# Linear attention block: the last VectorE step of a Q unit's feature map, issued in front of or behind the division of the token tile that follows it

## The chip, the cores and the metric

The kernel runs on one core of one Trainium2 chip. The metric is the device time of one launch in microseconds (us), the span of the core and the launch's own overhead together; the profile shows the span alone, some 1.8 us less.

## The reference, cut to what matters

```python
def _A_ref(x, wqkv, wo):                 # 32 heads of 32, S = 2048, D = 1024
    q, k, v = ...                        # x @ wqkv, split into heads
    phi = lambda t: jnp.where(t > 0, t + 1, jnp.exp(t)) + 1e-6
    pq, pk = phi(q), phi(k)
    kv = jnp.einsum("bhsd,bhse->bhde", pk, v)
    z = jnp.einsum("bhsd->bhd", pk)
    num = jnp.einsum("bhqd,bhde->bhqe", pq, kv)
    den = jnp.einsum("bhqd,bhd->bhq", pq, z)[..., None] + 1e-6
    return (num / den) ... @ wo
xn = layernorm(x)
out = x + _A_ref(xn, ...) * silu(swiglu_ffn(xn, w_gate, w_up, w_down))
```

## The kernel before

The kernel goes through three stages: K, V and the sums kv and z (0 to about 128 us); Q, the numerators and denominators, and the product with wo (128 to 250 us); then the SwiGLU part (250 to 762 us), which begins with the gate and up weights. The change is in the second stage. Its Q units (128 columns of q for 512 tokens, eight matmuls into one PSUM bank `q_ps`) belong to one of four blocks of 512 tokens, and their result goes through the feature map `emit_phi`. With `act=True`, three ScalarE activations are followed by one VectorE addition:

```python
def emit_phi(work, t_ps, dst, W, in_place=False, act=False):
    e_t = work.tile([P, W], FP32, name="e_t", tag="e_t")          # two buffers
    if act:
        nc.scalar.activation(out=e_t[:], in_=t_ps, func=ACT.Relu, scale=-1.0)
        nc.scalar.activation(out=e_t[:], in_=e_t[:], func=ACT.Exp, scale=-1.0)
        nc.scalar.activation(out=t_ps, in_=t_ps, func=ACT.Relu)
        nc.vector.scalar_tensor_tensor(out=dst, in0=e_t[:], scalar=EPS, in1=t_ps,
                                       op0=ALU.add, op1=ALU.add)
        return
    ...

def emit_Q(b, g):
    ...                                                     # eight matmuls into q_ps
    emit_phi(phiw, q_ps[:], pqT[:, g, :], TB, in_place=True, act=b > 0)
```

A token tile (128 tokens) takes eight short matmuls into `nd`, which holds numerators and denominators, and a division on VectorE. `nd` has one buffer of three PSUM banks, so the next tile's matmuls wait until this division has read it:

```python
def emit_ND(b, t, nd):
    for g in range(G):
        nc.tensor.matmul(nd[:, j, gi, :], lhsT=pqT[:, g, ttok], rhs=KVZ[:, g, :], ...)
    ...                                                     # two tensor_scalar: rden = den + EPS
    nc.vector.reciprocal(out=rden[:, 0:G, :], in_=rden[:, 0:G, :])
    for j in range(NJ):                                     # three multiplies: o_sb = nd * rden
        nc.vector.tensor_tensor(...)
```

The loop over blocks puts tiles among the Q units of the next block and the products with wo (`s_ps`) of the block before. In block 0 there is a tile after every second Q unit. `nd_item` in blocks 1 to 3 also carries a step of the weight preparation (on VectorE: `w_sb` times a power of two).

```python
for b in range(NB):
    q = [q_item(b + 1, g) for g in range(G)] if b + 1 < NB else []
    sl = sh(b - 1, 0) + sh(b - 1, 1) if b > 0 else []
    body = q[:2] + mix(q[2:], sl)
    at = (1, 4, 7, 10) if len(body) > 12 else ((1, 3, 5, 7) if b == 0 else (0, 2, 4, 6))
    for k, f in enumerate(body):
        f()
        if k in at:
            nd_item(b, at.index(k))()
```

In the third stage raw up-weights are loaded by DMA while the stage runs. Each is first read by a ScalarE activation that sums its squares, in the same ScalarE stream that empties the PSUM banks of the running products:

```python
def emit_st0(key, t):
    ...
    nc.scalar.activation(out=junk, in_=raw_view(key, t), func=ACT.Square, accum_out=asum[:])
...
load_w_to(...)                                              # step i of the up-weight loop
pipe(i + 4)                                                 # simplified: emit_st0 of a weight four steps ahead
if first and i in range(6, 11):
    io_load(mb)                                             # x and s for the output stage, 128 KB each
```

Of the kernel before, what the change touches and what calls it, by code (L numbers as in the profile page):

```python
# [10 lines left out]
ALU = mybir.AluOpType  # L11
# [10 lines left out]
def kernel(  # L22
# [11 lines left out]
    nc = tc.nc  # L34
# [24 lines left out]
    EPS = 1e-6  # L59
# [72 lines left out]
    hsc = persist.tile([P, 3], FP32, name="hsc")  # L132
    chs, rch, hmx = hsc[:, 0:1], hsc[:, 1:2], hsc[:, 2:3]

    def emit_phi(work, t_ps, dst, W, in_place=False, act=False):
        e_t = work.tile([P, W], FP32, name="e_t", tag="e_t")
        if act:
            nc.scalar.activation(out=e_t[:], in_=t_ps, func=ACT.Relu, scale=-1.0)
            nc.scalar.activation(out=e_t[:], in_=e_t[:], func=ACT.Exp, scale=-1.0)
            nc.scalar.activation(out=t_ps, in_=t_ps, func=ACT.Relu)  # L140
            nc.vector.scalar_tensor_tensor(out=dst, in0=e_t[:], scalar=EPS, in1=t_ps,
                                           op0=ALU.add, op1=ALU.add)
            return
        nc.scalar.activation(out=e_t[:], in_=t_ps, func=ACT.Exp)
        if in_place:
            r = t_ps
            nc.vector.tensor_scalar(out=r, in0=t_ps, scalar1=0.0, scalar2=EPS, op0=ALU.max, op1=ALU.add)  # L147
        else:
            r_t = work.tile([P, W], FP32, name="r_t", tag="r_t")
            r = r_t[:]  # L150
            nc.scalar.activation(out=r, in_=t_ps, func=ACT.Relu)
            nc.vector.tensor_scalar(out=r, in0=r, scalar1=EPS, scalar2=None, op0=ALU.add)
        nc.vector.scalar_tensor_tensor(out=dst, in0=e_t[:], scalar=1.0, in1=r,  # L153
                                       op0=ALU.min, op1=ALU.add)
# [8 lines left out]
    def emit_Q(b, g):  # L163
        if b not in pqT_tiles:
            pqT_tiles[b] = blk12.tile([P, G, TB], BF16, name="pqT", tag="pqT")
        pqT = pqT_tiles[b]
        btok = slice(b * TB, (b + 1) * TB)
        q_ps = ps2.tile([P, TB], FP32, name="q_ps", tag="B2")
        for dc in range(DC):
            nc.tensor.matmul(q_ps[:], lhsT=wq_sb[:, dc, g * P:(g + 1) * P], rhs=xn_ap(dc, btok),  # L170
                             start=(dc == 0), stop=(dc == DC - 1))
        emit_phi(phiw, q_ps[:], pqT[:, g, :], TB, in_place=True, act=b > 0)
# [136 lines left out]
    def prep_step(between=None):  # L309
        key = prep_q.popleft() if prep_q else None  # L310
        t = None
        if key is not None:
            t = w_slot()
            load_gu(t, key[1], key[2])
        if prep_out:
            emit_store(*prep_out.popleft(), nc.sync)
        k3 = prep_st.popleft()
        if prep_st[1] is not None:
            emit_st0(*prep_st[1])
        if k3 is not None:  # L320
            emit_st1(k3[0], stat_ps[0]())
        if between is not None:
            between()
        if k3 is not None:
            emit_st2(*k3)
            emit_T(*k3, later=True)
            prep_out.append(k3)
            if k3[0] in gkeys[0:2]:
                w_tiles[k3[0]] = k3[1]
        prep_st.append((key, t) if key is not None else None)  # L330
# [12 lines left out]
    def psa_tile(name):  # L343
        t = psA.tile([P, NJ, 512], FP32, name=name, tag="A")
        return t, t[:, :, 0:GPT * NDW].rearrange("p j (g c) -> p j g c", c=NDW)

    kvz_ps = psa_tile("kvz")[1]
    with ExitStack() as p1:
# [164 lines left out]
        def emit_Bev(i, c):  # L513
            kv_ps = kv_banks.pop((i, c))
            if i not in pkv_tiles:
                pk_sb = work.tile([P, D], BF16, name="pk_sb", tag="pk_sb")
                pkv_tiles[i] = (pk_sb, v_bufs[i % 2])
            pk_sb, v_sb = pkv_tiles[i]
            if c < NCC:
                emit_phi(phiw, kv_ps[:], pk_sb[:, c * CW:(c + 1) * CW], CW, in_place=i >= 9)  # L520
            else:
                vc = c - NCC
                nc.scalar.copy(out=v_sb[:, vc * GPC:(vc + 1) * GPC, 0:P],
                               in_=kv_ps[:].rearrange("p (g c) -> p g c", c=P))
# [78 lines left out]
        for j in range(NJ):  # L603
# [3 lines left out]
                                    in1=mask[:, None, :].to_broadcast([P, ng, P]), op=ALU.mult)  # L607
            nc.vector.tensor_tensor(out=KVZ[:, g0:g0 + ng, P:P + HPG],
                                    in0=kvz_ps[:, j, 0:ng, P:P + 1].to_broadcast([P, ng, HPG]),
                                    in1=sel[:, None, :].to_broadcast([P, ng, HPG]), op=ALU.mult)  # L610
# [23 lines left out]
    with ExitStack() as p2:  # L634
# [9 lines left out]
        def emit_ND(b, t, nd):  # L644
            pqT = pqT_tiles[b]
            ttok = slice(t * P, (t + 1) * P)
            if b not in o_blks:
                o_blks[b] = blk.tile([P, TPB, D], BF16, name="o_blk", tag="o_blk")
            o_sb = o_blks[b][:, t, :]
            for g in range(G):  # L650
                j, gi = divmod(g, GPT)
                nc.tensor.matmul(nd[:, j, gi, :], lhsT=pqT[:, g, ttok], rhs=KVZ[:, g, :], start=True, stop=True,  # L652
                                 skip_group_check=True)
            rden = small.tile([P, NJ * GPT, HPG], FP32, name="rden", tag="rden")
            for j0, j1, ng in ((0, NJ - 1, GPT), (NJ - 1, NJ, G - (NJ - 1) * GPT)):
                nc.vector.tensor_scalar(
                    out=rden[:, j0 * GPT:(j1 - 1) * GPT + ng, :].rearrange("p (j g) h -> p j g h", j=j1 - j0),
                    in0=nd[:, j0:j1, 0:ng, P:P + HPG], scalar1=EPS, scalar2=None, op0=ALU.add)
            nc.vector.reciprocal(out=rden[:, 0:G, :], in_=rden[:, 0:G, :])
            for j in range(NJ):  # L660
                g0 = j * GPT
                ng = min(GPT, G - g0)
                nc.vector.tensor_tensor(
                    out=o_sb[:, g0 * P:(g0 + ng) * P].rearrange("p (g h e) -> p g h e", g=ng, h=HPG),
                    in0=nd[:, j, 0:ng, 0:P].rearrange("p g (h e) -> p g h e", h=HPG),
                    in1=rden[:, g0:g0 + ng, :, None].to_broadcast([P, ng, HPG, DH]),
                    op=ALU.mult)

        def emit_OT(b, t):
            if t == 0:  # L670
                oT_tiles[b] = otp.tile([P, G, TB], BF16, name="oT", tag="oT")
            nc.sync.dma_start_transpose(out=oT_tiles[b][:, :, t * P:(t + 1) * P], in_=o_blks[b][:, t, :])
# [17 lines left out]
        def q_item(b, g):  # L690
            return lambda: emit_Q(b, g)
# [4 lines left out]
        def nd_item(b, t):  # L696
            def f():
                raw, nd = psa_tile("nd")

                def nd_ot():  # L700
                    emit_ND(b, t, nd)
                    emit_OT(b, t)
                if b > 0 and (b < NB - 1 or t % 2 == 0):
                    stat_ps[0] = lambda: raw[:, 0, 511:512]
                    prep_step(nd_ot)
                else:
                    nd_ot()
            return f

        def mix(a, b_):  # L710
            r = []
            for k in range(max(len(a), len(b_))):
                r += a[k:k + 1] + b_[k:k + 1]
            return r

        def sh(b, hf):
            return [s_item(b, t, cc) for t in (2 * hf, 2 * hf + 1) for cc in range(NCC)]
# [7 lines that stand above are left out]
                f()  # L725
                if k in at:
                    nd_item(b, at.index(k))()
        b = NB - 1
        blk_es.close()
        blk12_es.close()  # L730
# [519 lines left out]
```

## Time and profile before

Median 764.8 us of three runs (764.25 to 765.98); the profiled execution has a span of 762.1 us. Two lines of the page of the kernel before, its busy times by engine and the engines' shares of the chain that ended last:

```profile
...
PE 752.7 (99%) x3731; PEld 350.4 (46%) x3731; DVE 543.6 (71%) x1026; ACT 348.3 (46%) x479; POOL 269.1 (35%) x382
...
PE 94%; DVE 2%; DMA 1%; ACT 1%; issue 1%; SPq 0%; ACTq 0%; DVEq 0%
...
```

TensorE (PE) is busy practically always, and the chain is almost all PE. PE's busy time is no proof that it works at its peak; here what counts is that hardly any gap is left. The table of windows of the kernel before (each row: window, its length, busy time of PE, PEld, VectorE = DVE, ScalarE = ACT and GpSimd = POOL, granted clock, DMA share, GB/s):

```profile
...
core 0: us, PE busy (x) PEld busy (x) DVE busy (x) ACT busy (x) POOL busy (x), PEclk, DMA share, GB/s
145.00:166.00 21.00, 18.82 (x117) 9.30 (x115) 15.34 (x36) 16.57 (x30) 3.26 (x3) 1.00 0.40 82
166.00:240.00 74.00, 74.00 (x417) 36.41 (x416) 49.00 (x129) 54.06 (x86) 46.28 (x40) 1.00 0.93 262
...
```

From 166 to 240 us PE has no gap; between 145 and 166 us it lacks more than 2 us. The list of PE's waits of the kernel before (what waited, for what; total us, times, longest):

```profile
...
PE nd L652 <- DVE o_blk L663: 1.7, 2, 1.2
...
PE kv_ps L508 <- DMA wkv_sb<-in_A_wqkv_dram: 0.8, 1, 0.8
PE nd L652 <- DVE pqT L153: 0.4, 1, 0.4
...
```

The first line is the one that the change aims at. PE's own timeline of block 0 before (start, duration, line, operation, count; in brackets the idle time and what ended it). A row of 16 is two Q units, a row of 8 one tile:

```profile
...
147.01 3.62 PE L170 MATMUL q_ps<-xnT,wq_sb 128*128 128x512 bf16 x16
151.79 0.64 PE L652 MATMUL nd<-KVZ,pqT 128*128 128x132 bf16 x8 [1.17 <-DVE o_blk L663]
152.28 3.62 PE L170 MATMUL q_ps<-xnT,wq_sb 128*128 128x512 bf16 x16
...
156.20 3.62 PE L170 MATMUL q_ps<-xnT,wq_sb 128*128 128x512 bf16 x16
160.39 0.64 PE L652 MATMUL nd<-KVZ,pqT 128*128 128x132 bf16 x8 [0.58 <-DVE o_blk L663]
160.87 3.62 PE L170 MATMUL q_ps<-xnT,wq_sb 128*128 128x512 bf16 x16
...
```

Eight matmuls of a Q unit take 1.73 us and the eight of a tile 0.47, so the pairs could start 3.45 + 0.47 = 3.92 us apart. They start at 147.01, 152.28, 156.20, 160.87 and (not shown) 164.90. The first pair takes 5.27 us and so loses 1.35; its bracket shows only 1.17, because the row's end is modelled (3.62 us after its start), and the next matmul could have started after 3.45. VectorE's timeline over the first of these gaps (L141 is the addition, L656 to L663 the division):

```profile
...
147.45 0.69 DVE L141 SCALAR_TENSOR_TENSOR pqT<-e_t,q_ps 128x512 bf16<-128x512 f32 x1 [0.56 <-ACT q_ps L140]
149.11 0.69 DVE L141 SCALAR_TENSOR_TENSOR pqT<-e_t,q_ps 128x512 bf16<-128x512 f32 x1 [0.97 <-ACT q_ps L140]
149.71 0.25 DVE L656 TENSOR_SCALAR rden<-nd 128x24 f32<-128x24 f32 x2
...
150.38 1.35 DVE L663 TENSOR_TENSOR o_blk<-nd,rden 128x384 bf16<-128x384 f32 x3
151.65 0.68 DVE L141 SCALAR_TENSOR_TENSOR pqT<-e_t,q_ps 128x512 bf16<-128x512 f32 x1
```

The tile's matmuls had ended at 147.17 us (last one started 146.94, 0.23 us long), but its division starts at 149.71, right behind an addition for which VectorE had sat idle. The chain of waits in this stretch, followed back from PE, has the same story in order of time (start, duration, what):

```profile
...
147.35 0.59 ACT e_t L138
...
149.11 0.69 DVE pqT L141
149.80 0.17 DVE rden L656 x2
...
150.38 1.36 DVE o_blk L663 x3
...
151.79 0.64 PE nd L652 x8
...
```

| from the profile before | us |
|---|---|
| span | 762.1 |
| PE idle between 145 and 166 us | 2.18 |
| waits of nd on the division | 1.17 and 0.58 |
| one Q unit on ScalarE (three activations) | about 1.7 |
| the addition | 0.69 |
| the division, first start to the next instruction's start | 1.94 |

The Trainium skill, "Perfetto Trace Analysis", section "Optimization Strategy", says to look for the gaps of the engine in question and find the semaphore and the instruction that end them. That is what these views do; this trace bears it out, with the 1.17 us gap on the division leading to the addition's wait of 0.97 us for ScalarE.

### The profile page before, as it was taken

How to read it: one execution, taken by the hardware profiler on the slowest of the kernel's cores; microseconds unless marked ns; L12 is line 12 of the kernel's file. 1: busy time of each engine (PE TensorE's matmuls, PEld its weight loads, DVE VectorE, ACT ScalarE, POOL GpSimd, SP SyncE). 2: the span in 40 equal slices, each digit the busy share in tenths (PEclk: the TensorE clock that was granted, in tenths of full speed). 3: DMA queues.
4: the chain of work that ended last, by engine and by line, in shares of the span. 5: the costliest groups of instructions: out<-in, count | busy, mean ns of one | idle time of the engine just before them, and what ended most of it. 6: DMA issues, size and time to landing. Idle time of an engine off the chain costs nothing.

```text
span 762.1 us, 10455 instructions
## 1 busy us (share of the span) xinstructions
PE 752.7 (99%) x3731; PEld 350.4 (46%) x3731; DVE 543.6 (71%) x1026; ACT 348.3 (46%) x479; POOL 269.1 (35%) x382
## 2 busy tenths in 40 slices
PE   8999999999999999999999999999999999999997
PEld 3444444444444444444444444444444444444444
DVE  7788676876656588888889885358676767787335
ACT  4545777688853566666448411132323222211022
POOL 0577699708563255868655000110000000200000
PEclk9999999999999999999999999999999999999999
DMA  9986799669889769897887237398654445530824
GB/s 315 302 151 125 204 298 319 248 139 286 238 263 263 250 231 308 290 359 289 314 310 281 86 86 260 116 355 329 228 190 177 166 165 170 170 144 15 281 81 136
DMA packets 105908, 170.29 MB, mean 223 GB/s; under 512 B 34688, under 2 KB 82176, under 8 KB 95232
## 3 DMA queue, kind: packets, MB, share of 16 engines
q1 hardware_dynamic: 99280, 143.81, 59.9%
q0 software_dynamic: 3984, 21.24, 7.0%
q10 hardware_dynamic: 2592, 4.59, 1.8%
q8 instruction: 29, 0.48, 0.3%
q14 instruction: 23, 0.19, 0.1%
HBM read 111.67 MB, written 50.59 MB: 213 GB/s over the span
## 4 chain that ended last, share of the span: by engine, by line
PE 94%; DVE 2%; DMA 1%; ACT 1%; issue 1%; SPq 0%; ACTq 0%; DVEq 0%
PE zw L754 25%; PE kv_ps L508 14%; PE xb L754 13%; PE dzw L939 12%; PE s_ps L682 7%; PE yb L754 6%; PE dx L939 6%; PE q_ps L170 4%; PE dy L939 3%; DMA wkv_sb<-in_A_wqkv_dram 1%; PE kvz L530 1%; PE nd L652 1%; PE df L939 1%; DVE pqT L153 1%; DVE q_ps L147 1%
## 5 line engine op out<-in xcount | busy, mean ns | idle before, releaser
L754 PEld LDWEIGHTS <-w_sb 128*128 128x128 f16 (+1 forms) x1568 | 152.2, 98 | 182.9 <-issue 0.2
L508 PE MATMUL kv_ps<-wkv_sb,xnT 128*128 128x512 bf16 x512 | 113.7, 379 | 1.5 <-DMA wkv_sb<-in_A_wqkv_dram 0.8
L754 PE MATMUL xb<-xnT,w_sb 128*128 128x512 bf16 x448 | 115.0, 379 | 0.0
L754 PE MATMUL zw<-xnT,w_sb 128*128 128x512 bf16 x448 | 105.8, 379 | 0.0
L754 PE MATMUL zw<-S,w_sb 128*128 128x512 f16 x448 | 105.8, 379 | 0.0
L280 POOL TENSOR_TENSOR w_sb<-w_sb 128x512 f16<-128x512 bf16 x42 | 49.2, 1172 | 118.5 <-ACT s_sb L685 31.4
L247 ACT ACTIVATE w_sb<-w_sb 128x2048 bf16<-128x2048 bf16 x42 | 79.9, 1902 | 8.4 <-DMA w_sb<-in_B_w_up_dram 5.6
L939 PE MATMUL dx<-w_sb,hT 128*128 128x512 bf16 x210 | 79.6, 379 | 0.0
L508 PEld LDWEIGHTS <-xnT 128*128 128x128 bf16 x512 | 48.5, 97 | 57.1 <-issue 1.5
L939 PEld LDWEIGHTS <-hT 128*128 128x128 bf16 (+1 forms) x462 | 45.2, 98 | 51.7
L170 PE MATMUL q_ps<-xnT,wq_sb 128*128 128x512 bf16 x256 | 58.5, 379 | 0.2 <-DVE pqT L153 0.2
L939 PE MATMUL dzw<-w_sb,hT 128*128 128x512 f16 x196 | 58.3, 379 | 0.0
L682 PE MATMUL s_ps<-wo_sb,oT 128*128 128x512 bf16 x256 | 57.8, 379 | 0.0
L754 PE MATMUL yb<-S,w_sb 128*128 128x512 f16 x224 | 57.4, 378 | 0.0
L782 DVE SCALAR_TENSOR_TENSOR s<-yb,rc_all,s 128x512 f32<-128x512 f32 x42 | 31.5, 749 | 35.1 <-ACT s L781 35.0
L830 ACT ACTIVATE sg<-cg 128x1024 bf16<-128x1024 f32 x28 | 29.6, 1057 | 57.4 <-DVE cg L823 57.4
L823 DVE SCALAR_TENSOR_TENSOR cg<-zw,rc_all,s 128x1024 f32<-128x1024 f32 x28 | 35.9, 1284 | 25.9 <-PE zw L754 14.0
L283 POOL TENSOR_TENSOR w_sb<-w_sb 128x512 f16<-128x512 bf16 x42 | 50.8, 1210 | 0.0
L281 POOL TENSOR_TENSOR w_sb<-w_sb 128x512 f16<-128x512 bf16 x42 | 49.5, 1178 | 3.3
L282 POOL TENSOR_TENSOR w_sb<-w_sb 128x512 f16<-128x512 bf16 x42 | 50.3, 1198 | 0.0
L879 POOL TENSOR_TENSOR hs<-hT 128x512 f16<-128x512 bf16 x2 | 2.5, 1254 | 132.6 <-ACT sg L830 132.6
L913 POOL DMA_DIRECT2D out_dram<-io x16 | 8.7, 542 | 101.9 <-DVE io L912 101.6
(152 smaller groups left out, 1082.0 us busy)
## 6 DMA issues: line engine op xcount, KB each, us to landing
w_sb<-pk_g SPq DMA_DIRECT2D x27, 1024.0 KB, 5.6
pk_g<-w_sb SPq DMA_DIRECT2D x14, 1024.0 KB, 5.2
w_sb<-wd SPq DMA_DIRECT2D x14, 1024.0 KB, 5.0
w_sb<-pk_u SPq DMA_DIRECT2D x14, 1024.0 KB, 4.9
pk_u<-w_sb POOLq DMA_DIRECT2D x13, 1024.0 KB, 6.1
w_sb<-wd SPq DMA_DIRECT2D x14, 768.0 KB, 5.9
w_sb<-in_B_w_gate_dram SPq DMA_DIRECT2D x14, 512.0 KB, 6.4
w_sb<-in_B_w_down_dram SPq DMA_DIRECT2D x28, 256.0 KB, 3.9
```

Of the source, the lines that this page charges most:

```text
L170: nc.tensor.matmul(q_ps[:], lhsT=wq_sb[:, dc, g * P:(g + 1) * P], rhs=xn_ap(dc, btok), start=(dc == 0), stop=(dc == DC - 1))
L247: nc.scalar.activation(out=junk, in_=raw_view(key, t), func=ACT.Square, accum_out=asum[:])
L280: nc.gpsimd.tensor_tensor(out=T1, in0=b12, in1=b11, op=ALU.subtract)
L281: nc.gpsimd.tensor_tensor(out=T2, in0=b22, in1=T1, op=ALU.subtract)
L282: nc.gpsimd.tensor_tensor(out=T3, in0=b22, in1=b12, op=ALU.subtract)
L283: nc.gpsimd.tensor_tensor(out=T4, in0=b21, in1=T2, op=ALU.subtract)
L508: mm = nc.tensor.matmul(kv_ps[:], lhsT=xn_ap(dc, tok), rhs=wkv_sb[:, dc, c * CW:(c + 1) * CW], start=(dc == 0), stop=(dc == DC - 1))
L682: mm = nc.tensor.matmul(s_ps[:], lhsT=oT[:, c, ttok], rhs=wo_sb[:, c, cc * CW:(cc + 1) * CW], start=(c == 0), stop=(c == G - 1))
L754: mm = nc.tensor.matmul(out, lhsT=lhs(k), rhs=rhs(k), start=(first and k == 0), stop=(k == HK - 1), skip_group_check=True)
L782: nc.vector.scalar_tensor_tensor(out=s2[:], in0=y_[:], scalar=rc, in1=s1[:], op0=ALU.mult, op1=ALU.add)
L823: nc.vector.scalar_tensor_tensor(out=d12, in0=zw[:], scalar=rc, in1=s2[:, None, :].to_broadcast([P, 2, TB]), op0=ALU.mult, op1=ALU.add)
L939: nc.tensor.matmul(out, lhsT=lhs, rhs=rhs, start=first, stop=lastk, skip_group_check=True)
```

## The change

The addition of a Q unit that has a token tile right behind it is not issued at once, but after the tile's instructions. VectorE then finds a division that can start, in place of an addition that has to wait for ScalarE. For Q units without a tile behind them nothing changes.

```diff
+    phi_late = []
+
+    def phi_flush():
+        while phi_late:
+            phi_late.pop(0)()
+
     def emit_phi(work, t_ps, dst, W, in_place=False, act=False):
         ...
             nc.scalar.activation(out=t_ps, in_=t_ps, func=ACT.Relu)
-            nc.vector.scalar_tensor_tensor(out=dst, in0=e_t[:], scalar=EPS, in1=t_ps,
-                                           op0=ALU.add, op1=ALU.add)
+            phi_late.append(lambda: nc.vector.scalar_tensor_tensor(out=dst, in0=e_t[:], scalar=EPS, in1=t_ps,
+                                                                   op0=ALU.add, op1=ALU.add))
             return
 ...
             for k, f in enumerate(body):
                 f()
                 if k in at:
                     nd_item(b, at.index(k))()
+                phi_flush()
```

Ten of the 24 additions move: four in block 0, three each in blocks 1 and 2. The instruction order of the other engines and of the DMA queues is unchanged.

## The prediction

> **What bounds the kernel.** TensorE. The page's first part gives PE 752.7 us busy of a 762.1 us span (99%), VectorE 71%, ScalarE 46%. The chain that ended last is 94% PE and 2% VectorE. The table of windows shows PE solid (74.00 of 74 us, 270.00 of 270) from 166 us to 510 us. So only closing a PE gap can help. Within the change's reach the list of PE waits has nd on the division (o_blk), 1.17 and 0.58 us, both between 145 and 166 us, in the first attention block, where PE is busy 18.82 of 21 us.
>
> **What the change does.** Compared by instruction, the orders of PE, ScalarE, GpSimd and the DMA queues are unchanged; on VectorE ten of the 24 deferred additions (673 to 690 ns each) move: four in block 0, three in block 1, three in block 2. Each moves from in front of a token tile's division to behind it (in blocks 1 and 2 also behind the weight-scaling step). Nothing is added or removed. The timeline shows a division of 1.94 us (rden, reciprocal, three multiplies).
>
> **Why a gap closes.** The Trainium skill, "Perfetto Trace Analysis", section "Tensor Engine Instruction", says that VectorE is a strict FIFO; this trace agrees: the first nd ends at 147.17 us, but its division starts at 149.71 us, right behind an addition that sat 0.97 us for ScalarE's third activation. The division ends near 151.73 us, and nd has one PSUM buffer, so the next nd starts at 151.79 instead of 150.46. With the addition behind, the division should start at about 148.05 and release nd near 150.1, before PE asks for it. In steady state (estimated from these durations) the division starts 0.4 us after nd ends and finishes 2.4 us after; PE comes back 3.45 us after (two Q units at 1.73). So the later gap closes too.
>
> **Size.** PE's start-to-start period in block 0 should be 3.45 + 0.47 = 3.92 us. The trace shows starts of the Q pairs at 147.01, 152.28, 156.20, 160.87, 164.90: losses of 1.35 + 0.75 + about 0.1 us. Gain: about 2.1 us, once. Blocks 1 to 3 have no PE gap to close. The late additions should cost nothing: by the same reckoning the next user of their e_t buffer (two) comes just after, and the last one of block 0 is done near 161.9 us, while nd of block 1 would want it near 162.5 to 162.9.
>
> **Will it reach the end?** Weight preparation is ordered by PE and by buffers released by PE, so it should shift along. DMA is busy there (share above 0.9 from 166 to 215 us), but the first raw up-weights, issued at 243.94, are first read at 255.66, without waiting. Hence most of the 2.1 us arrives.
>
> **Predicted: 762.7 us (764.8 - 2.1); 761.6 to 764.4 in 8 of 10 cases. Faster by over 2%: 0.005; within 2%: 0.985; slower by over 2%: 0.01.**
>
> **What would show it.** PE's waits on o_blk vanish; PE is gapless from 147 to 166 us; the Q pairs start 3.92 us apart; the first division starts near 148.1; the first zw starts about 2.1 us earlier.
>
> **What would make it wrong.** A late addition holds an e_t buffer or a q_ps bank so that ScalarE, then PE, waits (a new PE wait on pqT or q_ps); or DMA-bound weight loads do not move with PE and a new wait on w_sb swallows the gain; or the run-to-run spread (764.25 to 765.98) hides 0.3%.

## The result, and the profile after

The changed kernel took 763.6 us (median of four runs, 762.58 to 764.01) and the kernel before, beside it, 764.52 us (four runs, 764.06 to 765.98); ratio 0.9983, 95% interval 0.9965 to 1.0. A ratio here is the mean time of one kernel's fast runs over that of the other's of the same rounds, so it is not quite the ratio of the medians quoted. The difference of the medians is 0.9 us, where 2.1 was predicted. The time lies in the predicted range, but that range reaches up to 764.4, almost to the time before, so lying in it proves little; what carries the argument is the stretches below.

PE's waits after the change:

```profile
...
PE kv_ps L514 <- DMA wkv_sb<-in_A_wqkv_dram: 1.3, 1, 1.3
PE zw L761 <- DVE cg L830: 0.7, 1, 0.7
PE nd L658 <- DVE pqT L159: 0.4, 1, 0.4
...
```

The wait on the division is gone and the small one on L159 (the addition of the earlier block, L153 before) stays. Two lines differ that the change was not meant to touch: 1.3 us for the first weights (0.8 before), and a new 0.7 us in the third stage. PE's timeline of block 0 after (some matmul records are missing from this trace, hence x15):

```profile
...
147.74 3.62 PE L176 MATMUL q_ps<-xnT,wq_sb 128*128 128x512 bf16 x16
151.19 0.63 PE L658 MATMUL nd<-KVZ,pqT 128*128 128x132 bf16 x8
151.67 3.62 PE L176 MATMUL q_ps<-xnT,wq_sb 128*128 128x512 bf16 x15
...
155.59 3.62 PE L176 MATMUL q_ps<-xnT,wq_sb 128*128 128x512 bf16 x16
...
159.51 3.61 PE L176 MATMUL q_ps<-xnT,wq_sb 128*128 128x512 bf16 x15
...
```

The pairs start at 147.74, 151.67, 155.59 and 159.51 us, 3.92 or 3.93 apart, without a gap. The table of windows for the same 21 us:

```profile
...
145.00:166.00 21.00, 20.48 (x124) 10.56 (x125) 17.86 (x45) 18.60 (x32) 3.92 (x4) 1.00 0.54 119
...
```

PE gained 1.66 us of work here. (That is less than the gap, since the window lies at a fixed time, this execution came to block 0 later, and some of its matmul records are missing.) VectorE after (L147 is the addition, L662 to L669 the division):

```profile
...
148.18 0.69 DVE L147 SCALAR_TENSOR_TENSOR pqT<-e_t,q_ps 128x512 bf16<-128x512 f32 x1 [0.56 <-ACT q_ps L146]
148.79 0.25 DVE L662 TENSOR_SCALAR rden<-nd 128x24 f32<-128x24 f32 x2
...
149.46 1.35 DVE L669 TENSOR_TENSOR o_blk<-nd,rden 128x384 bf16<-128x384 f32 x3
150.73 1.47 DVE L147 SCALAR_TENSOR_TENSOR pqT<-e_t,q_ps 128x512 bf16<-128x512 f32 x2
```

The first division starts 0.88 us after the tile's last matmul has ended (147.91, not shown), where it was 2.54 us before. The moved addition is done behind it, together with the next one (the row of two at 150.73).

So the gap is closed as intended, but the end of the run came only 0.5 us earlier in this pair of profiles (761.6 against 762.1). To see where, I cut each profile at four instructions: the last matmul of the first tile (nd), the first matmul of the third stage (yb), the first of the last part (dx), and the last group of matmuls (df).

| stretch, us | before | after | difference |
|---|---|---|---|
| start to nd | 146.94 | 147.68 | +0.74 |
| nd to yb (contains blocks 0 to 3) | 102.75 | 100.58 | -2.17 |
| yb to dx (gate and up weights) | 169.69 | 170.59 | +0.90 |
| dx to df | 332.44 | 332.46 | +0.02 |

The attention part gave 2.17 us. 0.74 us were lost before the change could act, and 0.90 us long after it. The second loss can be followed on ScalarE. Its timeline in the third stage, the two activations that first read one raw up-weight and the next, before the change:

```profile
...
325.56 1.91 ACT L247 ACTIVATE w_sb<-w_sb 128x2048 bf16<-128x2048 bf16 x1 [2.58 <-DMA w_sb<-in_B_w_up_dram]
...
336.85 1.91 ACT L247 ACTIVATE w_sb<-w_sb 128x2048 bf16<-128x2048 bf16 x1 [1.73 <-DMA w_sb<-in_B_w_up_dram]
...
```

And after it:

```profile
...
325.87 1.91 ACT L253 ACTIVATE w_sb<-w_sb 128x2048 bf16<-128x2048 bf16 x1 [4.33 <-DMA w_sb<-in_B_w_up_dram]
...
337.16 1.91 ACT L253 ACTIVATE w_sb<-w_sb 128x2048 bf16<-128x2048 bf16 x1 [3.43 <-POOL w_sb L288]
...
```

ScalarE waited 4.33 us instead of 2.58 us for the first of these tiles, and 3.43 instead of 1.73 for the second. PE shows no wait between the two, so the first delay was still within the slack of this execution. PE waited for `cg` at 345 us, behind the second, as the chain of waits up to there shows (start, duration, what; the first row is the end of the activation that directly follows the one at 337.16):

```profile
...
340.87 0.19 ACT w_sb L253
...
344.05 1.20 DVE cg L830
...
345.30 1.02 PE zw L761 x4
...
```

The profiles put the second wait down to DMA in some executions and to GpSimd (POOL) in others. It is DMA in all of them: wherever ScalarE waited for either of the two tiles, its activation starts 0.10 us after the tile's load landed.

### The profile page after: what moved, and what is told of

It reads as the page before. It is cut to its first block, busy times and chain, and to the rows that moved or that the text cites. A ratio compares the mean times of both kernels' runs of the same rounds, so it can differ in the third digit from the quotient of the medians.

```text
span 761.6 us, 10386 instructions
## 1 busy us (share of the span) xinstructions
PE 748.9 (98%) x3662; PEld 350.5 (46%) x3731; DVE 542.3 (71%) x1026; ACT 348.0 (46%) x479; POOL 269.6 (35%) x382
## 4 chain that ended last, share of the span: by engine, by line
PE 94%; DVE 3%; DMA 1%; issue 1%; ACT 0%; SPq 0%; DVEq 0%; ACTq 0%
PE zw L761 25%; PE kv_ps L514 14%; PE xb L761 12%; PE dzw L946 12%; PE s_ps L688 7%; PE yb L761 6%; PE dx L946 6%; PE q_ps L176 5%; PE dy L946 3%; DMA wkv_sb<-in_A_wqkv_dram 1%; PE nd L658 1%; PE kvz L536 1%; PE df L946 1%; DVE pqT L159 1%; DVE q_ps L153 1%
## 5 line engine op out<-in xcount | busy, mean ns | idle before, releaser
L761 PE MATMUL xb<-xnT,w_sb 128*128 128x512 bf16 x420 | 113.3, 379 | 1.5
L946 PE MATMUL dx<-w_sb,hT 128*128 128x512 bf16 x202 | 76.6, 379 | 0.3
L946 PE MATMUL dzw<-w_sb,hT 128*128 128x512 bf16 (+1 forms) x190 | 57.0, 379 | 0.0
L289 POOL TENSOR_TENSOR w_sb<-w_sb 128x512 f16<-128x512 bf16 x42 | 50.4, 1201 | 0.0
L288 POOL TENSOR_TENSOR w_sb<-w_sb 128x512 f16<-128x512 bf16 x42 | 50.4, 1199 | 0.0
```

The lines of the kernel that those rows point to most:

```text
L288: nc.gpsimd.tensor_tensor(out=T3, in0=b22, in1=b12, op=ALU.subtract)
L289: nc.gpsimd.tensor_tensor(out=T4, in0=b21, in1=T2, op=ALU.subtract)
L761: mm = nc.tensor.matmul(out, lhsT=lhs(k), rhs=rhs(k), start=(first and k == 0), stop=(k == HK - 1), skip_group_check=True)
L946: nc.tensor.matmul(out, lhsT=lhs, rhs=rhs, start=first, stop=lastk, skip_group_check=True)
```

## The experiments

Four theories about the missing gain came up, in this order:

- **A**: DMA sets a floor in the up-weight stage; a PE that comes earlier only waits there.
- **B**: both losses are chance.
- **C** (later C2): the additions moved in blocks 1 and 2 lengthen the up-weight stage, or make its slow transfers more frequent.
- **D** (later D2): the transfer times of raw up-weights vary from execution to execution, whatever the order on VectorE. At first I thought that such executions also show a late first weight load.

All runs were correct but one. "Before" in each set is the kernel before, run on the same chip in the same rounds.

### The full change again

No edit.

> The changed kernel once more, for a better interval and a second profile. In the first pair of profiles the changed kernel wins 2.17 us between the first nd and the first yb (102.75 to 100.58 us), but loses 0.74 us before the first nd (a late first weight load) and 0.90 us between the first yb and the first dx (169.69 to 170.59, with one wait of 0.65 us of zw on cg near 345 us). Theory A (a floor that DMA sets in the up-weight stage takes back what PE wins): the attention part wins 2.1 to 2.2 us again, and the first yb to the first dx again takes 0.4 to 1.0 us longer than before, with the same wait of zw on cg. Theory B (the losses are chance): the second profile shows about 169.7 us there and no such wait, and the median gain is 1.8 to 2.2 us. Timed under A: ratio 0.998 to 0.9988; under B: 0.997 to 0.9976.

Measured: 762.83 us median; ratio 0.9975 (0.9962 to 0.9988). Its profile fell in an execution of 1622 us, in which the matmuls took about twice as long (see the last section), and says nothing about this question. The four fast runs came at 761.84 to 762.9 us. Between A and B this decides nothing.

### Only block 0

```diff
                 f()
+                if b > 0:
+                    phi_flush()
                 if k in at:
                     nd_item(b, at.index(k))()
                 phi_flush()
```

> Only the four additions of block 0 go behind the division; those of blocks 1 and 2 stay as before. By my reasons the whole gain comes from block 0: the time from the first nd to the first yb is 100.5 to 100.7 us, as with the full change, and PE's waits on o_blk are gone. If the moves in blocks 1 and 2 mattered for the weight preparation, the stage from the first yb to the first dx would differ from the full change.

Measured: 761.82 us median, five of six runs between 761.74 and 762.01, one 764.61; ratio 0.9972 (0.9959 to 0.9986). nd to yb 100.58 us, waits on o_blk gone, yb to dx 169.69 us as before. The whole gain in the attention part comes from block 0. Theory A falls: this PE is just as early, measured from nd, and came to the first yb at 247.83 us, earlier than any profile so far, and did not wait.

### Only blocks 1 and 2

```diff
                 f()
+                if b == 0:
+                    phi_flush()
                 if k in at:
```

> Only the six additions of blocks 1 and 2 go behind the division. PE has no gap there, so nothing is gained: first nd to first yb 102.6 to 102.9 us as before, PE's two waits on o_blk (about 1.2 and 0.6 us) stay, ratio 0.9993 to 1.0007. If these moves help or hurt by themselves, the ratio is outside of that.

Measured: 764.92 us median (763.89 to 766.25); ratio 1.0005 (0.9993 to 1.0017). nd to yb 102.75 us and both waits on o_blk as before: no gain. But yb to dx was 170.04 us, with a wait of 0.17 us of zw on cg; as in the full change it came behind the second of the two up-weights, for which ScalarE had waited 2.92 us. This gave rise to theory C.

### The unchanged kernel under another name

No edit to the kernel before.

> The unchanged kernel under another name: the noise of the comparison and a second profile of it. Ratio 0.9993 to 1.0007. Under theory B the start up to the first nd varies by about 0.7 us from run to run (146.94 in the first profile) and the stage from the first yb to the first dx varies too; under theory A that stage is 169.7 us again, without a wait of zw on cg, since this kernel arrives later.

Measured: 764.08 us median (763.95 to 764.61); ratio 0.9996 (0.9984 to 1.0008). Start to nd 147.12 us, nd to yb 102.75, yb to dx 169.69. The ratio is 1 well within its interval, and the stretches from nd to yb and from yb to dx repeat exactly.

### The full change with late loads of x and s

```diff
-                if first and i in range(6, 11):
+                if first and i in range(20, 25):
                     io_load(mb)
```

> The changed kernel, with the five early loads of x and s for the output stage (ten of 128 KB) issued in steps 20 to 24 of the up-weight loop in place of steps 6 to 10, so that they no longer share the DMA with the raw up-weights between about 295 and 325 us. Theory D (the 0.90 us lost after the first yb is a slow DMA transfer of one raw up-weight tile, in executions in which the DMA is slow from the start, and not the moved additions): first yb to first dx is 169.7 us with no wait of zw on cg, whatever the start, and the median is 761.7 to 762.2 us. Theory C (the moves in blocks 1 and 2 cost time in that stage by themselves): the stage still takes 170.0 to 170.6 us, since the moves are still there.

Measured: 761.65 us median (761.49 to 762.36); ratio 0.9961 (0.9944 to 0.9977). nd to yb 100.58, yb to dx 169.69 us, no wait of PE in the third stage. ScalarE's timeline in this run, the same activation, now at 320.82 us and without a bracket, that is without idle time before it:

```profile
...
320.82 1.90 ACT L253 ACTIVATE w_sb<-w_sb 128x2048 bf16<-128x2048 bf16 x1
...
```

This activation no longer waits for DMA at all (the next one, at 334.80 us, still waits 1.75 us). With this, theory C in its first form falls: the moves in blocks 1 and 2 are still there, and the stage is as short as before. What they might still do is to use up slack that DMA lacks (C2).

### The kernel before with a shorter ScalarE chain (wrong on purpose)

The Q units that are issued in block 0 of the loop are those of block 1, hence `b == 1` in the edit.

```diff
-            nc.scalar.activation(out=t_ps, in_=t_ps, func=ACT.Relu)
+            if act != "short":
+                nc.scalar.activation(out=t_ps, in_=t_ps, func=ACT.Relu)
 ...
-        emit_phi(..., act=b > 0)
+        emit_phi(..., act="short" if b == 1 else b > 0)
```

> The kernel before, with the third activation left out of block 0's Q units: a wrong result on purpose. ScalarE's chain per unit falls from about 1.7 to 1.15 us, the order on VectorE stays as before. If the division was late because the addition in front of it waited for ScalarE, the first wait of nd on o_blk falls from 1.17 to below 0.3 us and the second vanishes; first nd to first yb is 100.6 to 101.0 us. If it was the work of the addition itself (0.69 us), most of the waits stay, at 102 us or more.

Measured: relative error 9.4, as intended; 763.5 us in its one run. The first wait fell from 1.17 to 0.61 us and the second is gone from the list (the pairs there start 4.19 us apart, so 0.27 us remain); nd to yb 101.70 us. That is half of the gain of the change, and between the two numbers that I had written down. VectorE's timeline shows why it is half:

```profile
...
147.01 0.69 DVE L142 SCALAR_TENSOR_TENSOR pqT<-e_t,q_ps 128x512 bf16<-128x512 f32 x1
148.60 0.69 DVE L142 SCALAR_TENSOR_TENSOR pqT<-e_t,q_ps 128x512 bf16<-128x512 f32 x1 [0.90 <-ACT e_t L139]
149.21 0.25 DVE L657 TENSOR_SCALAR rden<-nd 128x24 f32<-128x24 f32 x2
...
```

The work of the additions is the same 0.69 us, so what was gained came from waiting. But the second unit's addition still sat 0.90 us for ScalarE, since ScalarE began that unit hardly earlier than before (at 147.31 us, where it was 147.35), now after 0.33 us of idle time that the profile puts down to the tile's last matmul. So only the second unit's own chain became shorter: the division began 0.56 us earlier relative to the tile, about the pitch of the one activation left out. I had counted the shorter chain twice. The direction speaks for the wait as the cause; the size that I expected was wrong.

### Both additions of a pair behind the division

```diff
                 if k in at:
                     nd_item(b, at.index(k))()
-                phi_flush()
+                if b > 0 or k in at:
+                    phi_flush()
```

> As the full change, but in block 0 both additions of a pair go behind the division, so ScalarE gets its e_t buffers back later. By my reckoning there is margin: no new PE wait on pqT or q_ps, first nd to first yb 100.5 to 100.7 us. If the buffers have no margin, ScalarE waits for the addition, PE gets a wait on q_ps or pqT, and the time is 101 us or more.

Measured: nd to yb 100.59 us, the pairs 3.92 us apart, no wait of PE on the moved additions (L147). VectorE's timeline:

```profile
...
147.44 0.26 DVE L662 TENSOR_SCALAR rden<-nd 128x24 f32<-128x24 f32 x2 [0.33 <-PE nd L658]
...
148.11 1.35 DVE L669 TENSOR_TENSOR o_blk<-nd,rden 128x384 bf16<-128x384 f32 x3
149.38 1.27 DVE L147 SCALAR_TENSOR_TENSOR pqT<-e_t,q_ps 128x512 bf16<-128x512 f32 x2
...
```

Now the division waits only for the tile (0.33 us), and ScalarE does have to wait for its e_t buffer (0.86 us the first time, 0.52 us later); PE does not notice. So there is margin for the deferral, and no more to win in block 0: PE is without gaps already. This run too lost time in the third stage (yb to dx 171.59 us; ScalarE waited 6.16 us for DMA).

### The full change a third time

No edit.

> The changed kernel a third time, since the profile of the second fell in an execution at half the TensorE speed (1622 us). Theory C: first yb to first dx is 170.0 us or more again, also where the first nd comes at 147.3 us or earlier. Theory D: it is 169.7 us where the first nd comes by 147.3 us, and more only with a late first weight load (first nd at 147.6 us or later). Fastest timed run under D within 0.3 us of 761.8, the usual time of the kernel with only block 0 changed; under C above 762.4 in all runs but rare ones.

Measured: 762.83 us median (761.57 to 765.74); ratio 0.9978 (0.9958 to 0.9998). nd to yb is 100.58 us. The first nd came at 147.11 us, at the usual time, and yet yb to dx took 173.60 us. So the part of D that ties the loss to a late start is wrong. PE's waits in this profile:

```profile
...
PE xb L761 <- ACT sg L836: 1.1, 1, 1.1
...
PE yb L257 <- DVE s L789: 0.8, 1, 0.8
...
```

ScalarE's wait for the raw up-weight, the cause of both:

```profile
...
327.46 1.91 ACT L253 ACTIVATE w_sb<-w_sb 128x2048 bf16<-128x2048 bf16 x1 [6.49 <-DMA w_sb<-in_B_w_up_dram]
...
```

The chain of waits shows that the load itself was slow:

```profile
...
314.71 12.64 DMA w_sb<-in_B_w_up_dram
...
```

And the table of windows around it, the last row from a finer cut:

```profile
...
320.00:335.00 15.00, 13.10 (x59) 5.69 (x58) 10.94 (x20) 7.85 (x10) 5.08 (x5) 0.95 1.05 385
335.00:360.00 25.00, 25.00 (x116) 11.15 (x115) 19.58 (x32) 15.73 (x19) 21.85 (x22) 0.96 0.72 262
...
333.40:336.81 3.41, 3.41 (x10) 1.18 (x8) 2.31 (x7) 2.57 (x3) 1.56 (x2) 0.50 1.08 371
...
```

The two waits make 1.9 us of the 3.9 lost. The clocks of 0.95 and 0.96 are averages over one stretch of 3.41 us at half clock; at half speed it costs about 3.41 x 0.5 = 1.7 us (worked out from the last row), nearly all of the rest. The stretch begins 0.3 us after the second of the two waits ended. Whether the waits brought it on is not shown: two waits of 0.43 and 1.15 us at the same place in the kernel with both additions of a pair moved were followed by none. In the timed runs of this set the fastest was 761.57 us: the full change can run as fast as the best of the others, as D says.

### Only block 0 beside the full change

Two kernels already shown, without a further edit.

> Only block 0 changed, a second time. So far five of its six runs came at 761.7 to 762.0 us, and 14 runs of the full change spread from 761.6 to 765.7 with most near 763. Theory C2 (the moves in blocks 1 and 2 make the slow up-weight transfers more frequent): its median is again 0.7 us or more below that of the full change beside it, with most runs within 0.3 us of 761.8. Theory D2 (the transfers vary by chance, whatever the order on VectorE): the two medians lie within 0.4 us, with runs of both kernels on both sides. First nd to first yb is 100.58 us in any case.

> The full change beside it on the same chip. C2: median 762.5 to 763.2 us, spread over 1.5 us. D2: median within 0.4 us of the kernel with only block 0 changed. First nd to first yb 100.58 us; first yb to first dx 169.7 us where ScalarE's wait for the raw up-weight some 76 us after the first yb is below 3 us, and 0.3 to 2 us more where it is above 4 us.

Measured: only block 0, 762.22 us as reported over all six runs, the one at half speed included (median of the five fast ones 762.08, range 761.78 to 764.55), ratio 0.9975 (0.9962 to 0.9987); its profile fell in an execution with a span of 1336 us at little more than half the clock and is not used. The full change, 762.12 us (761.79 to 763.74), ratio 0.9973 (0.996 to 0.9986), nd to yb 100.58 us, yb to dx 170.89 us, with a PE wait of 1.04 us; ScalarE waited 5.46 us for the up-weight. In these rounds the two medians agree to 0.1 us, as D2 expected.

### Late loads with only block 0 changed, and with nothing changed

The edits of "only block 0" and of the late loads together; and the late loads alone.

> Only block 0 changed, and the early loads of x and s in steps 20 to 24: the best candidate. Both theories: 761.5 to 761.8 us in nearly all runs, first yb to first dx 169.7 us. Below the full change with late loads (761.65) by no more than 0.2 us, if the moves in blocks 1 and 2 do nothing once the DMA has room.

> The kernel before with the late loads: completes the square. If the late loads only take away the slow transfers, it runs at 763.7 to 764.0 us with fewer slow outliers, so the late loads give 0.1 to 0.6 us here, and the change gives 2.1 to 2.2 us on top of them (761.65 measured with both). PE's waits of nd on o_blk, 1.17 and 0.58 us, stay; first nd to first yb 102.75 us.

Measured: block 0 with late loads, 762.18 us (761.63 to 762.36), ratio 0.9968 (0.9956 to 0.998), nd to yb 100.58, yb to dx 169.69 us. Nothing changed but late loads, 764.34 us (763.85 to 764.67), ratio 0.9997 (0.9985 to 1.0009), nd to yb 102.75, yb to dx 169.69 us. Late loads alone give nothing measurable. On top of them the change in block 0 gives 764.34 - 762.18 = 2.16 us. As the best candidate it is not clearly better than the full change beside it (762.12): its median is no lower, only its spread is smaller. Two expectations were missed here: nearly all runs of this candidate at 761.5 to 761.8 us (two of five were), and 0.1 to 0.6 us from late loads alone.

### The profiles side by side

The up-weights are the two whose activations start near 325 and 337 us. All three times for them are in us.

| kernel of the profile | additions moved in blocks 1, 2 | loads | nd to yb | yb to dx | first up-weight, load from issue to landing | ScalarE's wait for it | ScalarE's wait for the second |
|---|---|---|---|---|---|---|---|
| before | no | early | 102.75 | 169.69 | 9.25 | 2.58 | 1.73 |
| before again | no | early | 102.75 | 169.69 | 9.58 | 2.68 | 1.97 |
| short ScalarE chain | no | early | 101.70 | 169.98 | 11.24 | 4.54 | 2.02 |
| only block 0 | no | early | 100.58 | 169.69 | 9.65 | 2.91 | 2.23 |
| only blocks 1, 2 | yes | early | 102.75 | 170.04 | 9.21 | 2.22 | 2.92 |
| full change | yes | early | 100.58 | 170.59 | 11.09 | 4.33 | 3.43 |
| full change, third time | yes | early | 100.58 | 173.60 (clock, see above) | 12.64 | 6.49 | 0.55 |
| full change, fourth time | yes | early | 100.58 | 170.89 | 12.17 | 5.46 | 2.29 |
| pairs | yes | early | 100.59 | 171.59 | 12.60 | 6.16 | 0.82 |
| full change | yes | late | 100.58 | 169.69 | 7.76 | none | 1.75 |
| only block 0 | no | late | 100.58 | 169.69 | 6.88 | none | 0.92 |
| before | no | late | 102.75 | 169.69 | 7.76 | none | 1.30 |

PE's time was lost behind the first up-weight in four profiles (short chain, third and fourth full change, pairs) and behind the second in two (only blocks 1 and 2, full change). The first load is issued 64.5 to 67.0 us after the first yb in all twelve; what differs is how long it takes: 9.2 to 12.6 us beside the loads of x and s, 6.9 to 7.8 us without them.

With early loads, the stage from yb to dx is longer than 169.7 us in all five profiles with moves in blocks 1 and 2, and in one of four without. In the timed runs 12 of 19 fast runs of the full change lie above 762.5 us, but only 2 of 11 of the kernel with only block 0 changed. The other kernels lean the same way: of all fast runs with early loads, 15 of 24 with moves in blocks 1 and 2, but only 15 of 53 without, lie more than 0.7 us above the fastest run of their kernel. On the other side stand the last set, where the two agree, and the short chain, which had no move and still waited 4.54 us; and the timed runs do not tell in which stage they lost. I also compared when the DMA queue issues its transfers in this stage, counted from the first yb, in eight of the nine profiles with early loads (all but the fourth of the full change). The issues at 50.4, 52.2 and 56.5 us agree to 0.1 us in all of them; they part afterwards (one at 64.7 to 65.6 us), among them the up-weight that comes late. So by then all stand alike, and I found nothing in the issue order that explains a difference. **Whether the moves in blocks 1 and 2 make the slow transfers more frequent stays open.** Settled is that they gain nothing, that a slow transfer also happened without them, and that none of the three profiles with late loads lost time in this stage.

## Why the prediction was right or wrong, point by point

- **TensorE bounds the kernel, and only a PE gap can be gained.** Right. Only block 0 had gaps, and only block 0 gave time.
- **The gap is an addition that waits for ScalarE in front of a division that could run.** Right. Moving it closes the gap, with the work on VectorE unchanged; shortening ScalarE's chain closes half of it; moving the additions of blocks 1 and 2 closes nothing.
- **Size: 2.1 us, pairs 3.92 us apart.** Right: 2.16 or 2.17 us from nd to yb in every profile with the additions of block 0 moved; pairs 3.92 to 3.95 us apart.
- **The division starts about 0.9 us after the tile and releases nd in time.** Right: 0.88 us. The absolute times given (148.05, 150.1) were late by the start of that execution.
- **The late additions cost nothing.** Right in block 0, and with margin: even both additions of a pair may go late.
- **Will it reach the end?** Here the prediction was too sure: "Hence most of the 2.1 us arrives." It argued from the raw up-weights issued just before the stage (one at 243.94 us), which were read 5.7 and 6.9 us after they had landed (loads and reads paired by their order). The tight ones come later. The trace before already showed them: ScalarE waited 2.58 us for DMA at 325 us and 1.73 us at 337 us. A wait in a trace without a PE gap says that the slack is being used, and I had read it as harmless. The first activation could start 1.74 us later than in the trace before, counted from the first yb, without a PE wait behind it (full change); 1.96 us later PE waited (short chain). The second could be 0.5 us later (only block 0), and 1.2 us later PE waited (only blocks 1 and 2). It was named among the things that could go wrong, but as a wait of PE on w_sb that comes of PE's being early; it was a wait on cg, sg or s, behind ScalarE, and it also came in an execution of a kernel whose block 0 was not changed.
- **The time.** 762.7 us was predicted; 763.6, 762.83, 762.83 and 762.12 us are the four medians, 0.9, 1.3, 1.6 and 2.1 us below the kernel before beside them. The first was above the prediction by 0.9 us; in its profiled execution 0.74 us went before nd, which is chance as far as the runs show, and 0.90 us to the slow transfers. That the number came out so close is partly luck: it started from 764.8 us, the median of three runs, where the later medians of the kernel before are 764.16 to 764.52, and this high start hid part of the gain that did not arrive.

## What to carry to other kernels

An engine that works its queue in order should not have an instruction that waits for a slow producer standing in front of one that is ready and frees a buffer that the bottleneck needs; issuing the first one later costs nothing as long as its own buffers have room, and the gain is read off beforehand from the start-to-start times of the bottleneck engine. Do it where the bottleneck has a gap; the same move elsewhere gains nothing. And before counting on the gain to reach the end, look for the stage behind it where another engine waits for DMA in front of emptying PSUM: even without a gap there yet, its slack is being used, and here the spread of its transfers decided how much arrived.

## What the Trainium skill lacked or had wrong

- **"TensorE: Matmul & The Clock Gate", "Back-to-back issue gap":** it gives about 131 ns per matmul of 512 columns as the sustained figure for a stream of weight loads and matmuls, and calls the 216 ns of its formula an isolated gap. In this kernel, with one weight load for every matmul, eight such matmuls take 1.73 us, 216 ns each, over hundreds of microseconds without a gap. Here the formula holds, and the sustained figure of this section does not.
- **The same page, "What's actually happening":** its table has two clock states, 4/8 and 8/8, and ties the low one to an idle window of some 3.4 us. Here one of 98 executions ran with a granted clock of 0.557, which is neither, and PE busy all the time. And the half clock of the third run of the full change came after PE waits of no more than 1.15 us each (that they caused it is not shown). The page of the slow execution (tenths of the clock in 40 slices):

```profile
...
PEclk6555555555555555555555555555555555555555
...
```

  Another had a span of 1622 us. The matmuls of 512 columns show 678 ns there, where 379 is usual. Its trace holds no clock record (its page has no PEclk row), so the clock of 1.00 that is listed for it was not measured, and what the clock was is not known. The line of a group in its page (busy, then mean ns of one):

```profile
...
L514 PE MATMUL kv_ps<-wkv_sb,xnT 128*128 128x512 bf16 x499 | 239.2, 678 | 3.2 <-issue 3.0
...
```

- **"DMA: Bandwidth & Descriptors", "Latency and other measured facts":** it has no spread for the time of one large transfer under load. Here 14 loads of 512 KB from the same tensor took 3.7 to 11.4 us from issue to landing (median 5.1) in one execution of the kernel before, and 3.6 to 12.6 (median 6.4) in one of the changed kernel (its third run); that spread decided how much of a gain arrived.
- **"Perfetto Trace Analysis", "Tensor Engine Instruction":** it says that VectorE and ScalarE are strict FIFOs, but no section draws the consequence that an instruction ready to run is held by the one in front, worth 2.17 us here, or that the order of issue is a means against it.
